# Letting the scheduler place two more elementwise steps on VectorE or GpSimd

## The chip, the cores and the metric

The kernel runs on one core of one Trainium2 chip. The metric is the device time of one execution in microseconds (us). The kernel before takes 389.71 us, the median of three runs (388.98 to 390.6). The profiled execution spans 388.5 us from its first to its last record, and all times read from the trace count from the start of that span.

The engines are named as in the profile: PE is TensorE, DVE is VectorE, ACT is ScalarE, POOL is GpSimd, and SP is the engine that issues most of the DMAs.

## The reference

Two parts follow each other. The first is attention in which a query sees only the keys of its own cluster. The second is a gated long convolution, computed in frequency space.

```python
# attention: B=4 batches, H=8 heads, S=768 positions, D=64
mask   = q_assign[:, :, :, None] == k_assign[:, :, None, :]   # nearest of 16 centroids
scores = scale * np.matmul(q, k.transpose(0, 1, 3, 2))
scores = np.where(mask, scores, -1e9)
attn   = softmax(scores)                                      # written out in the reference
x      = np.matmul(attn, v)                                   # heads joined to (B, S, 512)

# gated convolution ("hyena"), for each batch
proj = x @ w_proj                                             # 512 -> 3*512
x1, x2, x3 = proj[..., :D], proj[..., D:2*D], proj[..., 2*D:]
x2_conv = irfft(rfft(x2) * rfft(filter))                      # the spectral product
y = x1 * x2_conv * x3                                         # the product with the gates
out = y @ w_out
```

## The kernel before

The kernel doesn't write its instructions in program order. It first collects some 1,900 operations in a plan, each with the engines it may run on and a planned duration for each of them, with what it reads and writes and with a due time. A list scheduler then sends out the operations: it takes, for each engine, the operation that can start soonest, and among those that can start at about the same time the one with the earliest due time. The order in which operations are taken is the order of the instructions on each engine.

```python
def op(self, eng, fn, due, r=(), w=(), alloc=None, free=(), lock=False, ...):
    o.eng = eng if isinstance(eng, dict) else {eng[0]: eng[1]}    # {"POOL": 1.45, "DVE": .68} or ("DVE", .68)
    o.due += NUDGE.get(o.seq, 0.0)                                # a hand-set shift of single due times
    ...
```

An operation that may run on more than one engine has a dict of engines. `lock=True` marks the ones that the scheduler never lets overlap between DVE and POOL, in either direction:

```python
# place(): in choosing
if o.lock and e in ("POOL", "DVE"):
    t = late = max(t, st.dve if e == "POOL" else st.pool)
...
    c[1].due - (bonus if e == "PE" and st.kind == "pv" == c[1].kind else 0.0)
    + (shape if e == "PE" and array(c[1], st.last) != st.last else 0.0)
    + (BUSY if e == "DVE" and len(c[1].eng) > 1 else 0.0)         # DVE takes shared work later
...
# done(): after choosing
if e == "POOL" and o.lock: st.pool = t + d
if e == "DVE"  and o.lock: st.dve  = t + d
```

The attention is done in 16 passes, two for each of eight groups of four heads. A pass has six steps: PE makes scores, ACT takes their exponentials into one of five `p` buffers, PE multiplies with `v`, and DVE adds the exponentials up in `acc` for the softmax's denominators.

```python
op(("PE", 1.347), pv, due, r=[("p", slots[sk], u) for u in range(3)] + ..., w=[ob], kind="pv")
...
def acc(e, t=t):
    T.nc.vector.tensor_tensor(T.acc[os], P_(t[0]), P_(t[1]) if len(t) == 2 else T.acc[os], op=Alu.add)
op(("DVE", 1.75), acc, ..., w=[("acc", os)], lock=True)                          # L695
```

After most passes `acc` is folded from 128 rows to 16 by three DMAs that add on arrival. They are issued from POOL, one after the other. More DMAs then bring the sums into columns, DVE inverts them, and the inverses are spread to `rb`:

```python
while rows >= ROWS:
    op(("POOL", .8), lambda e, rows=rows: T.nc.gpsimd.dma_start(
        flat_()[:rows], flat_()[rows:2 * rows], accum_op=Alu.add), te, w=[("acc", os)], ...)   # L729
    rows //= 2
...                                                     # dd, dp, dn (DVE), dr, rb
op(("DVE", 1.05), ... scalar_tensor_tensor(xv(), osv(), eps(), rbv(), ...), w=[("xT", xs, kt)], lock=True)  # L775
```

Once a batch's `xT` is complete, its convolution ("hyena") is woven into the attention of later batches; that of the last batch comes after all attention. The parts that the change touches:

```python
def hyena(b):
    last = b == B - 1
    ...
    for i in range(3):
        for cs in range(2):                             # spectrum: PE into a bank h
            for r in range(2):                          # bank times filter, four products for each i
                op(("DVE", .68), ... tensor_tensor(T.tm[r][:, cs], ap(h), hmrow(...), op=Alu.mult), ...)     # L831
        for r in range(2):                              # sums of the spectral products
            op({"POOL": 1.45, "DVE": .68} if last and i < 2 else ("DVE", .68),
               lambda e, i=i, r=r: alu(e).tensor_tensor(
                T.y[:, i, r], T.tm[r][:, 0], T.tm[r][:, 1], op=Alu.add if r else Alu.subtract), due + 2,
               r=[("tm", r, 0), ("tm", r, 1)], w=[("y", i, r)], lock=True)                                    # L835
    ...
    for dt in range(4):
        ...                                             # gates on PE, x1 * x3 into x3 (ACT L260, DVE L871)
        ...                                             # inverse on PE, sums into sd (DVE L896), folded into yy (DVE L906)
        op(("DVE", .95), lambda e, dt=dt, x3=x3, yy=yy: alu(e).tensor_tensor(
            T.y2[:, dt], yy()..., x3()..., op=Alu.mult), due + 2.5, r=ykeys + xkeys,
            w=[("y2", dt)], lock=True)                  # L909, the product with the gates
    ...                                                 # y2 times w_out on PE, out to memory
```

There is one `tm[0]` and one `tm[1]`: the next products L831 can't be written before the sums L835 have read the last ones. `alu(e)` is the vector engine for "DVE" and GpSimd otherwise.

Of the kernel before, what the change touches and what calls it, by code (L numbers as in the profile page):

```python
# [22 lines left out]
B, H, S, D, NC = 4, 8, 768, 64, 16  # L23
# [9 lines left out]
NV = 3  # L33
NU = 4
ROWS = 16
LEAD = 1.97516
FIRST = 2
BUSY = 8.32578
HELD = 4
NUDGE = {10:3.7,75:-1.5,90:7.4,91:7.4,129:-0.8,140:0.4,156:6.6,187:-5.6,193:0.1,212:-0.2,216:15.5,218:8.0,222:-3.8,243:1.1,253:-4.1,255:-7.1,256:-7.1,257:-3.0,264:4.3,274:2.3,281:0.9,288:9.1,289:11.6,328:-9.2,363:0.5,370:2.2,378:0.5,379:0.7,400:-0.2,406:1.5,409:-4.8,434:0.6,440:-3.7,479:0.8,480:-0.3,481:-1.3,494:-0.6,495:-4.2,508:-1.9,511:-0.2,518:-5.0,524:0.5,526:2.1,539:-2.3,554:10.5,568:1.6,573:0.4,587:-4.9,590:0.2,597:-2.4,617:0.7,620:-1.0,658:0.8,664:0.1,684:2.2,690:-8.8,740:1.0,759:0.5,767:0.4,779:-0.7,782:1.7,788:0.7,790:0.8,826:-0.5,828:-0.3,848:-2.2,872:-1.3,883:-5.3,888:-3.6,897:-0.8,898:-1.1,901:-3.5,915:-3.1,941:0.4,947:-0.4,969:-0.8,996:2.0,997:2.0,1026:2.7,1029:-2.1,1039:2.0,1043:-1.2,1048:1.2,1056:10.8,1062:0.4,1066:0.9,1098:-1.0,1101:0.3,1118:-2.2,1127:1.5,1130:-1.5,1143:-2.6,1194:-0.9,1255:0.7,1257:0.7,1263:0.3,1270:-0.2,1271:-1.1,1276:-3.6,1295:4.9,1317:-2.0,1321:0.4,1351:5.6,1373:-1.5,1441:9.4,1450:3.5,1461:2.0,1478:-1.3,1501:-8.3,1546:0.2,1557:0.1,1563:-0.6,1624:2.8,1630:-1.5,1634:0.3,1640:-4.0,1641:-4.0,1642:-13.7,1643:-4.0,1655:-4.1,1666:0.5,1685:-2.9,1771:-3.3,1776:0.2,1788:-7.8,1797:0.1,1808:-0.1,1809:-0.1,1827:-0.7,1841:-1.3,1844:0.9,1862:-0.4,1863:2.1,1887:2.4,1890:3.2,1898:-7.4,1901:-0.8,1902:-1.5,1903:-0.8,1904:-0.8,1905:-1.8,1906:-1.8}  # L40
THIRDS = [[(0, 0, 512)], [(0, 512, 768), (1, 0, 256)], [(1, 256, 768)]]
HOLD = {"score": "score", "o": "o"}
AFTER = {"PE": .16}
# [32 lines left out]
class Plan:  # L76
# [6 lines left out]
    def op(self, eng, fn, due, r=(), w=(), alloc=None, free=(), lock=False, byts=0, after=(), kind=None, lat=0.0):  # L83
        o = Op()
        o.eng = eng if isinstance(eng, dict) else {eng[0]: eng[1]}
        o.fn, o.due, o.alloc, o.free, o.lock, o.byts, o.kind = fn, due, alloc, free, lock, byts, kind
        o.seq = len(self.ops)
        o.due += NUDGE.get(o.seq, 0.0)
        o.outs, o.end, o.start, o.on = [], None, None, None
        deps, o.soft = set(after), set(after)  # L90
        o.lat = lat
        for key in r:
            deps.update(self.writers.get(key, ()))
        for key in w:
            deps.update(self.writers.get(key, ()))
            deps.update(self.reads.get(key, ()))
        for key in r:
            self.reads.setdefault(key, []).append(o)
        for key in w:
            self.writers[key] = [o]  # L100
            self.reads[key] = []
        deps.discard(o)
        o.deps = deps
        o.left = len(deps)
        for d in deps:
            d.outs.append(o)
        for h in free:
            h.readers += 1
        self.ops.append(o)
        return o  # L110

    def place(self, free0, banks_for, switch=0.1, wait=0.1, rate=215e3, bonus=11.03330, margin=0.02203, shape=1.60501):
        free = dict(free0)
        bank_free = [0.0] * 8
        ready = {e: [] for e in free}
# [57 lines left out]
        while any(ready.values()):  # L173
# [28 lines left out]
            _, e, o, t = best  # L202
# [40 lines left out]
def build(T):  # L243

    P = Plan()
    op = P.op
    T0 = 20.36576
    TAU1 = 2.98452
    TAU2 = 3.43320
    NE = 28  # L250

    def ring(n, pr):
# [2 lines left out]
    def A(i):  # L255
        return T0 + TAU1 * min(i, NE) + TAU2 * max(i - NE, 0)

# [23 lines left out]
    def alu(e):  # L281
        return T.nc.vector if e == "DVE" else T.nc.gpsimd
# [253 lines left out]
    def routing(n):  # L536
        V = lambda: T.nc.vector
        g = n % 2
        end = A(12 * n)
        beg = A(12 * (n - 1)) if n else 0  # L540
        cls = "fill" if n > 1 else "head"
        for u in range(8):
# [7 lines left out]
            if n > 1 and ch == 0:  # L550
# [6 lines left out]
                for c in range(2):  # L557
                    op(EV384, lambda e, z=z, c=c, h=h: copy(e, T.qkT[z][:, c], bank(h.ids[c])[:, :384]), due + .9,
                       r=[h], w=[("qkT", z, c)], free=[h])
# [9 lines left out]
            if ch == 1:  # L569
                for hp in range(2):  # L570
# [3 lines left out]
                       r=[("qkT", z, 0), ("qkT", z, 1), ("zero", ring(n, pr), j)],  # L574
                       w=[("aug", ring(n, pr), hp, j)], lock=True)
        if n == 0:
            return got + first_masks(1)
        b0 = end - 24.00965
        h = Bank(cls, 2)

        def sim(e, h=h):
# [20 lines left out]
        for ch in range(2):  # L602
# [6 lines left out]
                op=Alu.is_equal), b0 + 3.4 + .2 * ch, r=[h, ("mx", ch)], w=[("oh", ch)], free=[h])  # L609
# [11 lines left out]
        for j, o_ in ((1, Alu.is_equal), (0, Alu.subtract)):  # L621
# [7 lines left out]
           r=both("oh"), w=both("ohT"), byts=196e3, lat=1.0)  # L629
# [153 lines left out]
    def hyena(b):  # L783
        xs = b % 2
        last = b == B - 1
        w0 = A(24 * (b + 1)) + 11.85069
        w1 = A(24 * (b + 2)) + 50.52404 if b < B - 2 else A(96) + 34.73131
        if last:
            w0 = A(96) - 8.47659
            w1 = w0 + 10  # L790
        acc = [0.0]

# [30 lines left out]
        for i in range(3):  # L823
            for cs in range(2):
                h = Bank()
                due = step(.66)
                op(("PE", .648), lambda e, i=i, cs=cs, h=h: spectrum(ap(h), i, cs), due,
                   r=[("uv2", e_, m) for m in range(3) for e_ in ((i,) if i < 2 else (0, 1))] + [("fw", m, cs) for m in range(3)],
                   w=[h], alloc=h, kind="proj" if i < 2 else "half")
                for r in range(2):  # L830
                    op(("DVE", .68), lambda e, i=i, cs=cs, r=r, h=h: T.nc.vector.tensor_tensor(  # L831
                        T.tm[r][:, cs], ap(h), hmrow(i, (0, 2, 2, 3)[2 * r + cs]), op=Alu.mult), due + 1 + .1 * r,
                       r=[h, ("hm", i, ((0, 2), (2, 3 if i == 0 else 0))[r][cs])], w=[("tm", r, cs), ("tm", r)], free=[h])
            for r in range(2):
                op({"POOL": 1.45, "DVE": .68} if last and i < 2 else ("DVE", .68), lambda e, i=i, r=r: alu(e).tensor_tensor(  # L835
                    T.y[:, i, r], T.tm[r][:, 0], T.tm[r][:, 1], op=Alu.add if r else Alu.subtract), due + 2, r=[("tm", r, 0), ("tm", r, 1)],
                   w=[("y", i, r)], lock=True)
        if last:
            op(("ACT", .83), lambda e: T.nc.scalar.activation(T.neg, T.inv[:, 1], Act.Copy, scale=-1.0), A(80),
               r=INV, w=["neg", ("qkraw", 0, 0), ("qkraw", 0, 1)])  # L840
        gs, inv = [], []
        for dt in range(ND):
            if last:
                x3, xkeys = (lambda dt=dt: T.qkT[dt][:]), [("qkT", dt, ch) for ch in range(2)]
            else:
                x3, xkeys = (lambda xb=dt % 2: T.x3[xb][:]), [("x3", dt % 2, ch) for ch in range(2)]
            if last and dt % 2:
                yy, ykeys = (lambda: T.sim[:].rearrange("p a (b c) -> p (a b) c", c=128)), [
                    ("sim", ch, pr) for ch in range(2) for pr in range(2)]
                od, okeys = (lambda: T.rb[:, :384]), [("rb", 0), ("rb", 1)]  # L850
            else:
                yy, ykeys = (lambda: T.yy[:]), [("yy", 0), ("yy", 1)]
                od, okeys = (lambda: T.od[:]), ["od"]
            sd, skeys = (lambda: T.sd[:]), [("sd", 0), ("sd", 1)]
            for ch in range(2):
                for off in (2 * DM, 0):
# [10 lines left out]
                    if off:  # L867
                        op(EV384, lambda e, ch=ch, x3=x3, h=h: copy(e, x3()[:, ch], ap(h)[:, :384]), due + .8,
                           r=[h], w=[xkeys[ch]], free=[h])
# [29 lines left out]
            for s_, o_ in ((0, Alu.add), (1, Alu.subtract)):  # L899
                def fold(e, s_=s_, o_=o_, yy=yy, sd=sd, hh=hh, od=od):  # L900
# [5 lines left out]
                    T.nc.vector.tensor_tensor(o[:, ::-1, 1, ::-1, ::-1] if s_ else o[:, :, 0], x[0], x[1], op=o_)  # L906
                op(("DVE", .55), fold, due + 2, r=[hh] + okeys if last else skeys, w=ykeys[s_::2], lock=not last,
                   free=[hh] if last else [])
            op(("DVE", .95), lambda e, dt=dt, x3=x3, yy=yy: alu(e).tensor_tensor(  # L909
                T.y2[:, dt], yy().rearrange("p t c -> p (t c)"), x3().rearrange("p a b -> p (a b)"),  # L910
                op=Alu.mult), due + 2.5, r=ykeys + xkeys, w=[("y2", dt)], lock=True)
        for tt in range(3):
# [261 lines left out]
```

The softmax here doesn't subtract the row's maximum and nothing guards it: scores larger than these inputs give would overflow.

## Time and profile before

| engine | busy us | share of the span | instructions |
|---|---|---|---|
| PE, matmuls | 369.0 | 95% | 3256 |
| PE, weight loads (beside the matmuls) | 214.3 | 55% | 3256 |
| DVE | 359.0 | 92% | 509 |
| ACT | 269.8 | 69% | 514 |
| POOL | 47.0 | 12% | 92 |

The TensorE clock is granted almost in full (0.998). Busy time is the union of an engine's instructions. A matmul's end is modelled, since matmuls overlap in the array, so the PE share says that matmuls were under way and not that the array was filled. The profile also follows one chain of work back from the end of the program; a piece of this chain is the work, or the wait, that the rest stood behind. Three stretches can be told apart: the start up to 20 us, attention with hyena woven in up to about 342 us, and after it the hyena of the last batch.

### The profile page before, as it was taken

What the parts mean: (1) busy time and instruction counts of PE and PEld (TensorE: products, weight loads), DVE (VectorE), ACT (ScalarE), POOL (GpSimd) and SP (SyncE); (2) the same over time, 40 slices, a digit from 0 to 9 for tenths busy, and PEclk for the clock granted to TensorE, in tenths of its full rate; (3) what the DMA queues carried; (4) which work ended last, traced back from release to release, by engine and by line L of the source; (5) the groups of instructions that cost most, each with busy time, mean ns of one, the idle gap of its engine ahead of it and who ended that gap; (6) DMA issues with size and microseconds to landing.
All of it is one profiled execution on the core that took longest, in us unless ns stands there. A gap on an engine that the chain in (4) does not pass through costs nothing.

```text
span 388.5 us, 8482 instructions
## 1 busy us (share of the span) xinstructions
PE 369.0 (95%) x3256; PEld 214.3 (55%) x3256; DVE 359.0 (92%) x509; ACT 269.8 (69%) x514; POOL 47.0 (12%) x92
## 2 busy tenths in 40 slices
PE   2999998999999999999999999999999999999995
PEld 1564454444445555555455554665454566557893
DVE  8898998899899999999899999999999999999782
ACT  5898687887884878787865976778865567632342
POOL 8502000000021010101010100101010100000400
PEclk9999999999999999999999999999999999999999
DMA  9819973740769759966897695745645651110214
GB/s 179 190 52 221 213 165 80 167 120 20 166 134 153 138 83 172 112 144 85 160 136 198 71 275 100 140 88 70 133 60 172 73 161 12 43 43 2 92 74 162
DMA packets 93860, 47.17 MB, mean 121 GB/s; under 512 B 82088, under 2 KB 87676, under 8 KB 93820
## 3 DMA queue, kind: packets, MB, share of 16 engines
q1 hardware_dynamic: 87836, 36.84, 41.6%
q0 software_dynamic: 2704, 8.98, 16.6%
q10 hardware_dynamic: 3280, 0.82, 1.2%
q8 instruction: 25, 0.41, 0.5%
q14 instruction: 15, 0.12, 0.1%
HBM read 31.59 MB, written 7.40 MB: 100 GB/s over the span
## 4 chain that ended last, share of the span: by engine, by line
PE 47%; DVE 35%; issue 7%; ACT 5%; DMA 3%; SPq 0%; DVEq 0%; POOL 0%; ACTq 0%; POOLq 0%
PE bank L73 17%; DVE acc L695 14%; PE pair L681 14%; PE bank L807 5%; PE bank L71 4%; DMA rb<-dr 2%; DVE oh L607 2%; PE bank L555 2%; DVE aug L262 2%; ACT p L670 2%; DVE tm L831 1%; PE bank L584 1%; DVE x L871 1%; ACT aug L260 1%; DVE mx L605 1%
## 5 line engine op out<-in xcount | busy, mean ns | idle before, releaser
L681 PE MATMUL pair<-p,vraw 128*64 128x385 f32 x768 | 142.9, 490 | 0.0
L670 ACT ACTIVATE p<-bank 128x512 f32<-128x512 f32 x192 | 113.7, 610 | 34.8 <-PE bank L73 33.3
L695 DVE TENSOR_TENSOR acc<-p,acc 128x1536 f32<-128x1536 f32 x64 | 111.9, 1749 | 3.5 <-ACT p L670 1.3
L681 PEld LDWEIGHTS pair<-p,vraw 128*64 128x64 f32 x768 | 54.0, 136 | 49.8 <-issue 45.2
L73 PE MATMUL bank<-aug,aug 80*64 80x512 bf16 (+3 forms) x590 | 69.7, 327 | 3.4 <-DVE den L717 1.0
L667 ACT ACTIVATE p<-bank 128x512 f32<-128x512 f32 x96 | 58.6, 610 | 2.7 <-PE bank L73 1.5
L73 PEld LDWEIGHTS <-aug 80*64 80x64 bf16 (+1 forms) x590 | 34.9, 109 | 34.7 <-issue 22.6
L729 POOL DMA_DIRECT2D acc<-acc x30 | 24.0, 799 | 245.5 <-DVE acc L695 85.4
L73 PE MATMUL bank<-xT,wpj 128*64 128x384 bf16 x424 | 41.4, 326 | 0.0
L260 ACT COPY qkT<-bank 128x384 f32<-128x384 f32 x62 | 27.9, 496 | 13.7 <-PE bank L73 8.9
L73 PEld LDWEIGHTS <-wpj 128*64 128x64 bf16 x424 | 27.9, 109 | 12.5 <-issue 6.7
L73 PEld LDWEIGHTS <-y 128*64 128x64 bf16 x448 | 24.9, 110 | 9.1 <-issue 3.0
L695 DVE TENSOR_TENSOR acc<-p,p 128x1536 f32<-128x1536 f32 x16 | 28.0, 1750 | 2.0 <-ACT p L670 2.0
L831 DVE TENSOR_TENSOR tm<-bank,hm 128x512 f32<-128x512 f32 x44 | 27.6, 677 | 0.8 <-ACT p L670 0.5
L260 ACT CAST aug<-qkT 64x768 bf16<-64x768 f32 x29 | 24.0, 829 | 3.0 <-PE bank L73 2.6
L807 PE MATMUL bank<-wpj,xT 128*64 128x512 bf16 x192 | 21.8, 380 | 0.4 <-DVE xT L775 0.4
L73 PE MATMUL bank<-wout,y 128*64 128x512 bf16 x176 | 21.4, 379 | 0.2 <-DVE y L909 0.2
L71 PE MATMUL bank<-aug,aug 80*128 80x256 bf16 (+3 forms) x89 | 19.9, 321 | 0.7 <-DVE tm L831 0.4
L555 PE MATMUL bank<-ident,qkraw 128*128 128x128 f32 x144 | 19.8, 279 | 0.2 <-DVE oh L607 0.2
L555 PEld LDWEIGHTS bank<-ident,qkraw 128*128 128x128 f32 x144 | 15.6, 140 | 7.1 <-issue 5.3
L260 ACT COPY tm<-bank 128x512 f32<-128x512 f32 x14 | 8.1, 590 | 16.1 <-PE bank L807 11.6
L262 DVE CAST aug<-qkT 64x768 bf16<-64x768 f32 x31 | 17.5, 569 | 1.5 <-PE bank L73 0.9
(149 smaller groups left out, 440.6 us busy)
## 6 DMA issues: line engine op xcount, KB each, us to landing
vraw<-in_v_dram SPq DMA_DIRECT2D x16, 384.0 KB, 4.3
qkraw<-in_q_dram SPq DMA_DIRECT2D x30, 192.0 KB, 5.0
qkraw<-in_k_dram SPq DMA_DIRECT2D x30, 192.0 KB, 5.1
rb<-dr SPq DMA_DIRECT2D x30, 192.0 KB, 3.7
out_dram<-ob SPq DMA_DIRECT2D x11, 512.0 KB, 3.6
acc<-acc POOLq DMA_DIRECT2D x10, 384.0 KB, 4.8
acc<-acc POOLq DMA_DIRECT2D x10, 192.0 KB, 4.0
y<-in_moe_filter_fft_dram SPq DMA_DIRECT2D x4, 384.0 KB, 6.8
```

The source lines that it names most:

```text
L71: return T.nc.tensor.matmul(out, lhsT, rhs, start=start, stop=stop)
L73: T.nc.tensor.matmul(out[64 * i:64 * i + 64], lhsT[:, 64 * i:64 * i + 64], rhs, start=start, stop=stop)
L260: T.nc.scalar.copy(out, in_)
L262: (T.nc.vector if e == "DVE" else T.nc.gpsimd).tensor_copy(out, in_)
L555: T.nc.tensor.transpose(bank(h.ids[i // 3])[:, ts(i % 3, 128)], raw(s, i), T.ident)
L667: T.nc.scalar.activation(o, ap(h).rearrange("p (a b) -> p a b", a=2), Act.Exp, scale=0.125)
L670: T.nc.scalar.activation(flat(s)[:, lo:lo + 512], ap(h), Act.Exp, scale=0.125)
L681: T.nc.tensor.matmul(o[64 * hp:64 * hp + 64, ch, :385], T.vraw[vs][:, hp, sk * D:(sk + 1) * D], T.p[slots[sk]][:, hp, 384 * ch:384 * ch + ...
L695: T.nc.vector.tensor_tensor(T.acc[os], P_(t[0]), P_(t[1]) if len(t) == 2 else T.acc[os], op=Alu.add)
L729: op(("POOL", .8), lambda e, rows=rows: T.nc.gpsimd.dma_start(flat_()[:rows], flat_()[rows:2 * rows], accum_op=Alu.add), te, r=[], w=[("ac ...
L807: T.nc.tensor.matmul(ap(h)[64 * i:64 * i + 64], T.xT[xs][:, kt, c:c + 64], T.wpj[:, kt, DM:2 * DM], start=kt == 0, stop=kt == ND - 1)
L831: op(("DVE", .68), lambda e, i=i, cs=cs, r=r, h=h: T.nc.vector.tensor_tensor(T.tm[r][:, cs], ap(h), hmrow(i, (0, 2, 2, 3)[2 * r + cs]), op ...
```

## The change

Two kinds of operations get GpSimd as a second possible engine. These are the sums of the spectral products (L835), before only in the last batch, now in all others too, and the products with the gates (L909) in all batches but the last. The purpose is to take elementwise work off VectorE where GpSimd has time. The scheduler decides instance by instance, by its planned durations.

The scheduler's constants and the hand-set due times were set anew along with it. The list of shifted due times grows from 142 to 420 operations; 121 of the old entries keep their value. No computation is added or left out.

```diff
-LEAD = 1.97516
+LEAD = 2.11573
-BUSY = 8.32578
+BUSY = 9.78676
-NUDGE = {10:3.7,75:-1.5,90:7.4, ... (142 entries) }
+NUDGE = {10:3.7,11:0.5,19:3.3, ... (420 entries) }
-    def place(self, ..., bonus=11.03330, margin=0.02203, shape=1.60501):
+    def place(self, ..., bonus=11.38616, margin=0.02203, shape=1.67099):
-    T0 = 20.36576
-    TAU1 = 2.98452
-    TAU2 = 3.43320
+    T0 = 20.37328
+    TAU1 = 2.98605
+    TAU2 = 3.41134
-        b0 = end - 24.00965
+        b0 = end - 24.14381
-        w0 = A(24 * (b + 1)) + 11.85069
-        w1 = A(24 * (b + 2)) + 50.52404 if b < B - 2 else A(96) + 34.73131
+        w0 = A(24 * (b + 1)) + 11.20895
+        w1 = A(24 * (b + 2)) + 50.66493 if b < B - 2 else A(96) + 36.68989
-            w0 = A(96) - 8.47659
+            w0 = A(96) - 9.51087
...
-                op({"POOL": 1.45, "DVE": .68} if last and i < 2 else ("DVE", .68), lambda e, i=i, r=r: alu(e).tensor_tensor(
+                op({"POOL": 1.45, "DVE": .68} if last and i < 2 or not last else ("DVE", .68), lambda e, i=i, r=r: alu(e).tensor_tensor(
                     T.y[:, i, r], T.tm[r][:, 0], T.tm[r][:, 1], op=Alu.add if r else Alu.subtract), ...
...
-            op(("DVE", .95), lambda e, dt=dt, x3=x3, yy=yy: alu(e).tensor_tensor(
+            op({"DVE": .95, "POOL": 2.2} if not last else ("DVE", .95), lambda e, dt=dt, x3=x3, yy=yy: alu(e).tensor_tensor(
                 T.y2[:, dt], ...
```

## The prediction

> **What bounds the kernel now.** I read the page's busy lines and its 40 slices first, then the busy times by stretch, then the groups of instructions, and last the chain that ended last.
>
> ```profile
> PE 369.0 (95%) x3256; PEld 214.3 (55%) x3256; DVE 359.0 (92%) x509; ACT 269.8 (69%) x514; POOL 47.0 (12%) x92
> ...
> PE   2999998999999999999999999999999999999995
> PEld 1564454444445555555455554665454566557893
> DVE  8898998899899999999899999999999999999782
> ACT  5898687887884878787865976778865567632342
> POOL 8502000000021010101010100101010100000400
> ```
>
> Two engines are nearly full at once, PE and DVE, and POOL is nearly empty from 20 us on. The busy times by stretch (start and end in us, length, then busy us and instructions of PE, weight loads, DVE, ACT and POOL) say where there is room:
>
> ```profile
> 20.00:120.00 100.00, 96.47 (x774) 49.32 (x772) 91.38 (x114) 81.22 (x156) 5.25 (x8) 1.00 0.62 133
> 120.00:300.00 180.00, 176.73 (x1494) 98.61 (x1492) 174.42 (x242) 133.52 (x252) 20.77 (x26) 1.00 0.71 130
> 300.00:340.00 40.00, 40.00 (x396) 24.16 (x394) 38.35 (x54) 25.32 (x49) 1.52 (x2) 1.00 0.39 78
> 340.00:380.00 40.00, 39.59 (x498) 32.56 (x496) 35.88 (x60) 13.74 (x27) 5.01 (x4) 1.00 0.15 51
> ```
>
> The operations of the change run from 129 us, where the first sums stand, to 342 us. Up to 120 us PE stands idle for 3.5 us that this change can hardly reach. From 120 to 300 us PE stands idle for 180 - 176.7 = 3.3 us, and from 300 to 340 us not at all. That is the visible room. The chain shows that there is also hidden room. From 220 to 240 us PE is counted as busy for 20.00 of 20 us, and yet the chain runs over DVE there (start us, us, what):
>
> ```profile
> 225.14 0.68 DVE tm L831
> 225.82 1.67 DVE acc L695
> 227.48 1.20 DVE tm L831 x2
> 228.68 0.45 DVE y L835
> 229.13 0.07 issue
> 229.20 0.68 DVE y L835
> 229.88 0.59 DVE acc L695
> 230.47 1.00 issue
> ```
>
> So DVE does set the pace in places, and the sums L835 are among the pieces. Over the whole span the chain is 47% PE and 35% DVE, which is 136 us of DVE. A busy PE with the chain on DVE means that matmuls trickle and their modelled ends cover the gaps.
>
> **What the Trainium skill says.** "Perfetto Trace Analysis", Identifying the Most-Contended Engine, says that matmul busy time is no good measure of how near PE is to its limit, while occupancy is a fair one for VectorE. The trace agrees: PE reads 100% busy from 220 to 240 us with weight loads at 10.33 us of 20, against 32.56 us of 40 from 340 to 380 us. "GPSIMD Engine Reference", Performance versus the Vector engine, gives a two-input add as 1.96 times slower there. The trace has the same sum on both engines, 1272 ns against 676, a factor of 1.88. "SBUF — State Buffer", Who interferes with whom, says that a VectorE instruction with two SBUF inputs contends with a GpSimd instruction that reads SBUF, and that the second to start waits in full. Nothing in this trace shows that pair: the four sums on POOL lie beside products of DVE that read a bank, and these kept their 0.68 us. It matters here, since the additions into `acc` have two SBUF inputs.
>
> **The change part by part.** The order of the built program tells how many operations really move. Before, 4 sums stood on POOL; after it is 22, so 18 leave DVE. Of the 12 products with the gates outside the last batch 6 go to POOL. Casts of `aug` on DVE fall from 31 to 24 (they go to ACT), copies of `inv` from 4 to 2, and ten copies from banks come to DVE (3 of 512 columns, 7 of 384). The matmuls are the same, and the changes between column layouts of the array number 86 against 82. Durations from the groups (busy us, mean ns):
>
> ```profile
> L835 DVE TENSOR_TENSOR y<-tm 128x512 bf16<-128x512 f32 x20 | 13.0, 676 | 0.0
> L909 DVE TENSOR_TENSOR y<-yy,x 128x768 bf16<-128x768 f32 x12 | 11.5, 958 | 0.5
> L835 POOL TENSOR_TENSOR y<-tm 128x512 bf16<-128x512 f32 x4 | 5.0, 1272 | 49.8 <-DVE tm L831 49.8
> ```
>
> With the means of the same view for the casts and copies, DVE loses 18 x 0.676 = 12.2 us of sums, 6 x 0.958 = 5.7 us of products, 7 x 0.569 = 4.0 us of casts and 2 x 0.25 = 0.5 us of `inv`: 22.4 us. It gains 3 x 0.692 + 7 x 0.541 = 5.9 us. Net DVE goes from 359.0 to about 342.5 us. POOL gains 18 x 1.27 = 22.9 us and, at 1.27/512 us a column, 6 x 1.9 = 11.4 us: 47 + 34 = 81 us. ACT gains 7 x 0.83 = 5.8 us of casts and gives back about as much in copies.
>
> What of the 17 us is on the path? The moved kinds have these larger pieces in the chain: sums 0.66 us at 129, 0.45 and 0.68 us at 229, 0.60 us at 317; products 0.96 us at 172, 0.97 us at 292, 0.64 us at 325. That is 5.0 us. Nearly all sums move and half of the products, so I count the sums in full (2.4 us) and half of the products (1.3 us): 3.7 us. The other 13 us lie beside PE's work; they only let a later addition into `acc`, an evacuation or a cast start sooner. PE's room caps what that can bring: 3.3 us visible from 120 to 300 us plus some hidden, and I count 2 us for it, my choice.
>
> Against it: a sum on POOL ends 1.27 - 0.68 = 0.6 us later and a product 1.9 - 0.96 = 0.95 us later. Each of three batches waits for its last sum before its inverse transform and for its last product before the output matmul. If half of this is covered, it is 3 x (0.6 + 0.95) / 2 = 2.3 us of delay on PE inputs, but PE has attention to do meanwhile, so I count 0.8 us. And where a POOL instruction meets an addition into `acc`, one waits: 24 times a chance that the schedule mostly avoids; I count 0.5 us. Sum: 389.7 - 3.7 - 2.0 + 0.8 + 0.5 = 385.3 us.
>
> **Rivals.** First, nothing moves, since PE is the bound. For it speaks that PE is 95% busy and full from 300 to 340 us, and that the attention's additions into `acc` (two groups of 111.9 and 28.0 us) stay on DVE. Against it speaks the chain on DVE. It would give 388 to 390 us. Second, a new wait on POOL: the three folding DMAs of `acc` are issued from the same POOL queue, in order, and in the new order sums stand between a first fold and its second, waiting for DVE's products. The folds, the spreading and `xT` then come later; the chain already holds 2% of the span in the wait for `rb`. Together with the shared port this could cost 2 to 6 us: 391 to 395 us. Against it: `acc` has two buffers, and the scheduler plans both the queue and the lock. Third, the 278 newly shifted due times are what really pays: the order is repacked everywhere, up to 120 us too. Then the gain could reach the whole idle time of PE in the middle and part of the hidden: 380 to 382 us. The shifts can't be priced from a profile of the old order; that they come with a shorter planned step (TAU2 3.411 for 3.433) says only that the order is meant to be tighter.
>
> **Range and chances.** The cap is PE: 369 us busy plus what nothing fills, 7.8 us in the first 20 and 4.4 us in the last 8.5, makes 381.2 us unless hidden gaps close as well. Faster by over 2% needs less than 381.9 us, nearly the cap, and so gets 0.16. Slower by over 2% needs 397.5 us, beyond the second rival: 0.04. The rest is 0.80. The range is 380.5 to 390.0 us: the third rival below, the first above.
>
> **What would show it.** Right: DVE near 342 us busy and POOL near 80; PE busy within 3 us of 369 with less idle time from 120 to 300 us; hardly any L835 among the chain's pieces before 342 us; additions into `acc` still near 1.75 us. Wrong: additions into `acc` or sums on POOL clearly longer than 1.75 and 1.27 us (the port); more time waiting for `rb` or for POOL (the queue); a gain that lies mostly before 120 us, or a PE busy time lower by over 4 us (the repacked order, and hidden gaps larger than I count).

## The result, and the profile after

The changed kernel takes 394.24 us (median; 393.62 to 396.57), the kernel before 389.92 us in the same set of runs. The ratio is 1.0123 with a 95% interval of 1.0077 to 1.017: about 1.2% slower, where the prediction had 385.3 us and a range of 380.5 to 390.0. The profiled execution spans 392.6 us against 388.5.

The page's busy lines and three of its 40-slice lines:

```profile
PE 370.1 (94%) x3281; PEld 210.1 (54%) x3281; DVE 354.8 (90%) x485; ACT 273.1 (70%) x514; POOL 85.5 (22%) x116
...
PE   2999998999999999898999999999998999999995
...
DVE  8898998896999999979999899999996999999882
...
POOL 8501100000020741401010350401021170501500
```

The move took place: DVE has 24 instructions fewer and POOL 24 more, and POOL's busy time rose by 38.5 us. But DVE's busy time fell only from 359.0 to 354.8 us. The prediction's count of instructions would have taken it to about 342.5. The busy times by stretch (columns as before: start:end, length, then busy us and instructions of PE, weight loads, DVE, ACT and POOL) show that PE did not close its gaps either:

```profile
20.00:120.00 100.00, 96.98 (x775) 52.18 (x773) 89.43 (x108) 83.89 (x162) 5.13 (x8) 1.00 0.61 133
120.00:300.00 180.00, 174.81 (x1494) 98.80 (x1492) 170.67 (x226) 134.69 (x249) 44.19 (x40) 1.00 0.68 125
300.00:340.00 40.00, 38.08 (x374) 21.27 (x372) 35.73 (x48) 22.92 (x44) 11.69 (x10) 1.00 0.46 100
340.00:380.00 40.00, 39.88 (x501) 26.16 (x497) 36.51 (x58) 14.32 (x29) 10.05 (x6) 1.00 0.14 51
```

From 120 to 300 us PE stands idle for 5.2 us (3.3 before), from 300 to 340 us for 1.9 us (none before). The attention's last pass ends on PE at 346.2 us instead of 342.3; what follows takes as long as before (46.4 and 46.2 us). So the loss lies where the moved operations lie, between 120 and 342 us.

The groups of instructions tell where DVE's relief went (busy us and mean ns of one after the bar, then the idle time before them and what ended it):

```profile
L695 DVE TENSOR_TENSOR acc<-p,acc 128x1536 f32<-128x1536 f32 x64 | 116.9, 1826 | 3.7 <-ACT p L670 1.1
...
L695 DVE TENSOR_TENSOR acc<-p,p 128x1536 f32<-128x1536 f32 x16 | 30.1, 1880 | 4.4 <-ACT p L667 3.9 <-ACT p L670 0.4
...
L835 POOL TENSOR_TENSOR y<-tm 128x512 bf16<-128x512 f32 x22 | 29.6, 1372 | 23.5 <-DVE tm L831 23.5
...
L775 DVE SCALAR_TENSOR_TENSOR xT<-osb,rb 128x768 bf16<-128x768 f32 x15 | 16.7, 1115 | 5.2 <-DMA rb<-dr 5.2
...
L909 POOL TENSOR_TENSOR y<-yy,x 128x768 bf16<-128x768 f32 x6 | 15.1, 2524 | 41.6 <-DVE yy L906 27.6 <-PE bank L807 14.0
...
L740 DVE TENSOR_SCALAR dn<-dn 128x12 f32<-128x12 f32 x10 | 4.7, 468 | 0.3
```

Before, the same groups of DVE were:

```profile
L695 DVE TENSOR_TENSOR acc<-p,acc 128x1536 f32<-128x1536 f32 x64 | 111.9, 1749 | 3.5 <-ACT p L670 1.3
...
L695 DVE TENSOR_TENSOR acc<-p,p 128x1536 f32<-128x1536 f32 x16 | 28.0, 1750 | 2.0 <-ACT p L670 2.0
...
L775 DVE SCALAR_TENSOR_TENSOR xT<-osb,rb 128x768 bf16<-128x768 f32 x15 | 15.1, 1006 | 1.3 <-DMA rb<-dr 1.3
...
L740 DVE TENSOR_SCALAR dn<-dn 128x12 f32<-128x12 f32 x10 | 1.7, 173 | 0.3
```

The same instructions on the same data now last longer: 7.0 us more for the additions into `acc`, 3.0 us for L740, 1.6 us for L775, together 11.5 us. A mean hides the form of this: most of these instructions are as long as before, and 13 single ones carry the whole 11.5 us (8 of the 80 additions, 4 of L740, 1 of L775). Each of them starts while an elementwise operation stands on POOL. The timeline around 230 us (start us, us, engine, line) shows two such meetings:

```profile
227.77 1.31 DVE L831 TENSOR_TENSOR tm<-bank,hm 128x512 f32<-128x512 f32 x2
...
228.85 1.50 POOL L835 TENSOR_TENSOR y<-tm 128x512 bf16<-128x512 f32 x1
228.99 2.98 DVE L695 TENSOR_TENSOR acc<-p,p 128x1536 f32<-128x1536 f32 x1
231.89 0.68 DVE L831 TENSOR_TENSOR tm<-bank,hm 128x512 f32<-128x512 f32 x1
...
232.74 1.27 POOL L835 TENSOR_TENSOR y<-tm 128x512 bf16<-128x512 f32 x1 [2.40 <-DVE tm L831]
232.96 2.67 DVE L695 TENSOR_TENSOR acc<-p,acc 128x1536 f32<-128x1536 f32 x1
```

The sum on POOL runs from 232.74 to 234.01 us. The addition of 232.96 ends at 235.63, that is 1.62 us after the sum has ended, against 1.75 us for an undisturbed addition: it stood still behind the sum and then ran nearly as if it began there. The products L831 read a bank, and keep their 0.68 us beside POOL. The case of 292 us is the clearest. L740 works on 12 elements a row and takes 0.17 us alone:

```profile
292.49 1.82 POOL L909 TENSOR_TENSOR y<-yy,x 128x768 bf16<-128x768 f32 x1 [7.15 <-DVE yy L906]
292.77 1.56 DVE L740 TENSOR_SCALAR dn<-dn 128x12 f32<-128x12 f32 x1
```

It ends at 294.33 us, just after the product has ended at 294.31. The chain of waits shows the price of the second addition (start us, us, what):

```profile
233.03 0.59 DVE acc L695
233.63 1.92 issue
```

In the chain of before, shown with the prediction, the same pair of pieces was 0.59 and 1.00 us. The second has grown by 0.92 us, and this addition lasts 0.92 us longer than the mean of before. The blocked time is not named: it goes under "issue", the time for which the profile shows no reason.

### The profile page after: what moved, and what is told of

It reads as the page before. It is cut to its first block, busy times and chain, and to the rows that moved or that the text cites. A ratio compares the mean times of both kernels' runs of the same rounds, so it can differ in the third digit from the quotient of the medians.

```text
span 392.6 us, 8528 instructions
## 1 busy us (share of the span) xinstructions
PE 370.1 (94%) x3281; PEld 210.1 (54%) x3281; DVE 354.8 (90%) x485; ACT 273.1 (70%) x514; POOL 85.5 (22%) x116
## 4 chain that ended last, share of the span: by engine, by line
PE 70%; DVE 16%; ACT 5%; DMA 4%; issue 3%; SPq 1%; POOL 0%; DVEq 0%; POOLq 0%; ACTq 0%
PE bank L73 27%; PE pair L681 24%; PE bank L807 5%; PE bank L71 3%; DVE acc L695 3%; PE bank L555 3%; DMA rb<-dr 2%; PE bank L584 2%; DVE oh L607 2%; PE bank L450 2%; ACT p L670 1%; DVE mx L605 1%; DMA dp<-dd 1%; PE bank L565 1%; PE bank L709 1%
## 5 line engine op out<-in xcount | busy, mean ns | idle before, releaser
L670 ACT ACTIVATE p<-bank 128x512 f32<-128x512 f32 x192 | 111.6, 606 | 29.2 <-PE bank L73 26.5
L695 DVE TENSOR_TENSOR acc<-p,acc 128x1536 f32<-128x1536 f32 x64 | 116.9, 1826 | 3.7 <-ACT p L670 1.1
L73 PE MATMUL bank<-aug,aug 80*64 80x256 bf16 (+3 forms) x584 | 68.9, 327 | 4.3 <-DMA aug<-ohT 1.8
L667 ACT ACTIVATE p<-bank 128x512 f32<-128x512 f32 x96 | 58.1, 606 | 5.7 <-PE bank L73 5.1
L835 POOL TENSOR_TENSOR y<-tm 128x512 bf16<-128x512 f32 x22 | 29.6, 1372 | 23.5 <-DVE tm L831 23.5
L695 DVE TENSOR_TENSOR acc<-p,p 128x1536 f32<-128x1536 f32 x16 | 30.1, 1880 | 4.4 <-ACT p L667 3.9
L73 PEld LDWEIGHTS <-wpj 128*64 128x64 bf16 x424 | 24.4, 109 | 15.9 <-issue 6.9
L260 ACT CAST aug<-qkT 64x768 bf16<-64x768 f32 x36 | 29.8, 830 | 3.0 <-PE bank L73 1.2
L831 DVE TENSOR_TENSOR tm<-bank,hm 128x512 f32<-128x512 f32 x44 | 27.7, 680 | 1.7 <-POOL y L835 0.7
L909 POOL TENSOR_TENSOR y<-yy,x 128x768 bf16<-128x768 f32 x6 | 15.1, 2524 | 41.6 <-DVE yy L906 27.6
L71 PE MATMUL bank<-aug,aug 128*128 128x512 bf16 (+3 forms) x92 | 20.6, 323 | 1.8 <-DVE x L262 1.0
L775 DVE SCALAR_TENSOR_TENSOR xT<-osb,rb 128x768 bf16<-128x768 f32 x15 | 16.7, 1115 | 5.2 <-DMA rb<-dr 5.2
```

The source lines that it names most:

```text
L71: return T.nc.tensor.matmul(out, lhsT, rhs, start=start, stop=stop)
L73: T.nc.tensor.matmul(out[64 * i:64 * i + 64], lhsT[:, 64 * i:64 * i + 64], rhs, start=start, stop=stop)
L260: T.nc.scalar.copy(out, in_)
L667: T.nc.scalar.activation(o, ap(h).rearrange("p (a b) -> p a b", a=2), Act.Exp, scale=0.125)
L670: T.nc.scalar.activation(flat(s)[:, lo:lo + 512], ap(h), Act.Exp, scale=0.125)
L835: op({"POOL": 1.45, "DVE": .68} if last and i < 2 or not last else ("DVE", .68), lambda e, i=i, r=r: alu(e).tensor_tensor(T.y[:, i, r], T. ...
```

## The experiments

One theory (the port theory) stood against three rivals. The theory: GpSimd's reads of SBUF block DVE, and the blocking eats the relief. The rivals: the new order of instructions is at fault; or the fuller POOL queue delays the folds of `acc` and so `rb`; or the relief of DVE is worth nothing in itself because PE or another wait takes over. Every ratio below is against the kernel before in the same set of runs, without the executions that took over 1.5% longer than the fastest of their kernel.

### Reads or writes on GpSimd, in the new order

The order and the engines of every instruction are those of the changed kernel. The 24 moved operations are replaced by two fills, which only write, between two reads of a single column. The sums and products themselves are left out.

```diff
+def wonly(e, o, x, z, f):                       # o = x f z
+    if last or e == "DVE": return alu(e).tensor_tensor(o, x, z, op=f)
+    n = o.shape[-1]
+    T.nc.gpsimd.tensor_tensor(o[:, :1], x[:, :1], z[:, :1], op=f)
+    for _ in range(2): T.nc.gpsimd.memset(o[:, 1:n - 1], 0.0)
+    T.nc.gpsimd.tensor_tensor(o[:, n - 1:], x[:, n - 1:], z[:, n - 1:], op=f)
-    alu(e).tensor_tensor(T.y[:, i, r], ...)     # L835, and L909 likewise
+    wonly(e, T.y[:, i, r], ...)
```

> The changed kernel in its own order, but each of the 24 moved operations on GpSimd is replaced by a read of one column, two writes of a constant over the rest, and a read of the last column. The queue stays as occupied and the waits stay; only the long reads of SBUF by GpSimd are gone, and with them the sums and products themselves. Port theory (GpSimd's reads and VectorE's two-input instructions hold each other up): additions into acc back to 1750 ns in the mean, the 11.5 us of lengthened VectorE instructions gone, time 385 to 389 us. Queue theory (operations on GpSimd delay the folding DMAs behind them): nothing changes, 392 to 396 us. Order theory (the newly set due times are themselves worse on the chip): nothing changes, 392 to 396 us.

Measured: 392.4 us, a ratio of 1.0037 (1.0014 to 1.0059). The profiled execution is a quick one of this kernel (its span is 387.5 us), so its trace is used for durations only. DVE is busy for 345.0 us, within 2.5 us of what the prediction's count said. The port theory's time, 385 to 389 us, was missed; its lengths came out. The additions are back at their old length although POOL, at 90.8 us, is even busier:

```profile
L695 DVE TENSOR_TENSOR acc<-p,acc 128x1536 f32<-128x1536 f32 x64 | 112.0, 1750 | 5.7 <-ACT p L670 3.3
```

Its timeline near the same place shows a fill beside an addition:

```profile
226.28 1.23 POOL L803 MEMSET y<- 128x510 bf16 x2
226.57 1.75 DVE L695 TENSOR_TENSOR acc<-p,p 128x1536 f32<-128x1536 f32 x1
227.47 0.91 POOL L804 TENSOR_TENSOR y<-tm 128x1 bf16<-128x1 f32 x1
...
229.00 0.19 POOL L801 TENSOR_TENSOR y<-tm 128x1 bf16<-128x1 f32 x1 [0.63 <-DVE tm L840]
```

The addition of 226.57 us overlaps the fills and takes 1.75 us. The read of one column that follows the fills, 0.19 us when alone, takes 0.91 us: it waits for the end of the addition at 228.32. Of the 11.5 us of lengthening, 0.8 us is left: four of the ten L740 still take 0.30 to 0.58 us beside fills (a mean of 254 ns for 173). So fills spare the additions, not every DVE instruction. The two ratios, 1.0123 and 1.0037, have intervals that don't overlap; their difference, 0.86% or 3.4 us, is what the long reads of SBUF on GpSimd cost. "SBUF — State Buffer", Who interferes with whom, of the Trainium skill says exactly this: a VectorE instruction with two SBUF inputs contends with a GpSimd instruction that reads SBUF and not with one that only writes, and the second to start is blocked in full. These runs agree: beside a read an addition took 2.98 us, beside fills 1.75.

### The new order with everything on VectorE

```diff
-alu(e).tensor_tensor(T.y[:, i, r], ...)                               # L835, and L909 likewise
+(alu(e) if last else T.nc.vector).tensor_tensor(T.y[:, i, r], ...)
```

The order is again that of the changed kernel; the moved operations stand at their planned places, on DVE.

> The changed kernel with every instruction where it stands, but the 24 moved operations are issued on VectorE at the same place of the order. Port theory: VectorE gets 17 us of work back and loses 11.5 us of stalls, so 392 to 396 us, with the additions at 1750 ns. Queue theory: the folds start as soon as their data are there, 387 to 391 us. Order theory: VectorE is now fuller than the order was made for, 396 to 402 us.

Measured: 396.7 us, 1.0169 (1.0132 to 1.0205), just above the port theory's 392 to 396 us and within the order theory's range; DVE 358.6 us busy, additions 1749 ns. So in this order the relief is worth something: from 1.0169 to 1.0037 it is 1.3%, 5.1 us, if it is had without the blocking. With it 0.5% is left (1.0123), and the intervals overlap. But this order was made for 24 instructions less on DVE. Against the kernel before, the order with its relief and without the blocking is still not ahead.

### The new constants and due times alone

```diff
-LEAD = 1.97516; BUSY = 8.32578; NUDGE = {... 142 entries}; TAU2 = 3.43320; ...
+LEAD = 2.11573; BUSY = 9.78676; NUDGE = {... 420 entries}; TAU2 = 3.41134; ...
```

The engine options stay those of before; the scheduler makes a new order.

> All constants and shifted due times of the changed kernel, but the sums and products may only go where they could before, so the scheduler makes a new order with them on VectorE. Port and queue theories: no loss remains, 386 to 390 us. Order theory: the loss remains, 393 us or more.

Measured: 404.06 us, 1.0356 (1.0313 to 1.0399). Two lines of its busy times by stretch:

```profile
340.00:380.00 40.00, 35.76 (x451) 27.87 (x448) 33.21 (x53) 9.69 (x20) 5.01 (x4) 0.96 0.04 11
380.00:402.00 22.00, 13.82 (x112) 6.47 (x108) 8.01 (x12) 6.04 (x11) 0.00 (x0) 0.88 0.37 144
```

The last pass ends on PE at 343.0 us, within a microsecond of the kernel before. The loss lies almost all behind it, where the last batch's operations take 58.0 us instead of 46.2, PE is idle for 4.2 of 40 us, and the granted clock (the column after POOL's) is lower. That is a place that the options don't touch. The run therefore doesn't weigh the new due times for the changed kernel. It shows only that the scheduler's order with these due times and the old engines is slow in another place.

### The two options alone

```diff
-{"POOL": 1.45, "DVE": .68} if last and i < 2 else ("DVE", .68)
+{"POOL": 1.45, "DVE": .68} if last and i < 2 or not last else ("DVE", .68)   # L835
-("DVE", .95)
+{"DVE": .95, "POOL": 2.2} if not last else ("DVE", .95)                      # L909
```

Constants and due times stay those of before. The scheduler puts 17 more sums and 6 products on POOL.

> The kernel before with its own constants and due times; only the two operations may go to GpSimd as in the change (21 sums and 6 products end there). Port theory: VectorE instructions are lengthened by 8 to 13 us in all, 391 to 396 us. Queue theory: 391 to 396 us, with a longer wait for rb. Order theory: no loss, 385 to 389 us.

Measured: 394.5 us, 1.0108 (1.0076 to 1.014), as slow as the full change. The lengthening is there again (1838 ns for the first additions, 1119 for L775, 469 for L740), with an order that shares neither constants nor due times with the changed kernel. It comes to about 6 us, less than the 8 to 13 expected; but DVE's products L831 here also wait 4.0 us for POOL to read `tm` (0.3 us before), so this run does not set the two apart.

### The old order, writes only and real

The order of the kernel before is kept to the instruction. The 18 sums of the first three batches and every second product are issued on POOL at their places: once as fills, as above (sums and products left out), and once in earnest.

```diff
-alu(e).tensor_tensor(T.y[:, i, r], ...)                        # L835
+wonly(e if last else "POOL", T.y[:, i, r], ...)                # fills
-alu(e).tensor_tensor(T.y2[:, dt], ...)                         # L909
+wonly(e if last or dt % 2 else "POOL", T.y2[:, dt], ...)
```

The second kernel has `alu(e if ... else "POOL").tensor_tensor` in place of `wonly`.

> The order of the kernel before on every engine, untouched; its 18 sums of the first three batches and 6 of the products leave VectorE and become, on GpSimd, the read of one column, two writes of a constant and the read of the last column. VectorE is relieved by 18 x 0.676 + 6 x 0.958 = 17.9 us and the port is left alone; the sums and products are left out. If relief is worth something in the old order (the prediction's step): 385 to 388 us. If PE or the order leave no room for it: 389 to 391 us.

> The order of the kernel before on every engine, untouched; the same 18 sums and 6 products are really computed on GpSimd. Port theory: VectorE instructions are lengthened by 10 to 16 us in all, since this order was not made for it (most sums are followed by an addition into acc), and the time is 3 to 6 us above that of the kernel with writes only in the old order: 390 to 395 us. If the newly set order is the cause of the loss and not the port: 385 to 388 us.

Measured: 390.92 us for the fills, 1.0009 (0.9989 to 1.003), and 395.12 us in earnest, 1.015 (1.0091 to 1.021). The blocking costs 1.4%, about 5.5 us, in the old order; the additions last 1812 and 1844 ns and L775 1189 ns.

The first of these is the more telling one. The fills take 14 us off DVE's busy time and leave the additions alone, and the time stays where it was. Its busy line, and the 120 to 300 us of its busy times by stretch:

```profile
PE 368.5 (95%) x3256; PEld 206.7 (53%) x3256; DVE 345.0 (89%) x485; ACT 269.8 (69%) x514; POOL 88.7 (23%) x188
```

```profile
120.00:300.00 180.00, 176.06 (x1492) 97.16 (x1488) 164.45 (x226) 132.94 (x252) 48.04 (x90) 1.00 0.69 128
```

DVE is busy for 164.45 us of the 180 instead of 174.42, and PE for 176.06 instead of 176.73. The 10 us of relief became 10 us of idle time. DVE's waits name more than half of it. Over the whole span, before and with the fills (what waited, for what: us in all, times, longest):

```profile
DVE tm L831 <- POOL y L835: 0.3, 1, 0.3
...
DVE tm L840 <- POOL y L804: 8.8, 9, 1.4
```

L840 and L804 are the products L831 and the last read of a sum in the file of this kernel. There is one `tm`, so after each of the nine groups of sums DVE's next products wait until POOL has read it. In this order, which has those products close behind, 8.8 of the 14 us came back as a wait for POOL; 5.8 of them fall between 120 and 300 us. With the real sums the wait is 8.1 us, so the comparison of the two kernels still shows the blocking. In the changed kernel it is 0.7 us.

The shares of the chain, before, by engine:

```profile
PE 47%; DVE 35%; issue 7%; ACT 5%; DMA 3%; SPq 0%; DVEq 0%; POOL 0%; ACTq 0%; POOLq 0%
```

With the fills:

```profile
PE 61%; DVE 23%; issue 4%; ACT 3%; DMA 3%; POOL 2%; SPq 1%; DVEq 0%; POOLq 0%; ACTq 0%
```

DVE lost 12 points of the chain and PE gained 14, at the same time. POOL's 2% are the fills themselves: 4.7 us from 128 us on and 2.7 us from 310 us on, where the chain of before had 0.66 and 0.60 us of sums on DVE. The first piece is a read of one column (0.19 us alone) that ends just after an addition of DVE from 128.78 to 130.52 us:

```profile
128.35 2.23 POOL y L801
```

So this order shows what the move is worth in it even without blocked additions, nothing, and not what 14 us less on DVE would be worth if nothing else had become late.

DVE's wait for `rb` is 3.7 us here against 1.3 before. Without the waits for `rb`, further down, the kernel with fills is 0.5% faster (1.0009 to 0.996) and the one without them 0.2%. So a price of the fuller queue is not ruled out. For the changed kernel the fills show that 3.4 us of its loss go while the queue stays as full.

### One kind at a time, in the new order

```diff
-alu(e).tensor_tensor(T.y2[:, dt], ...)          # products back on DVE: sums alone move
+alu("DVE").tensor_tensor(T.y2[:, dt], ...)
-alu(e).tensor_tensor(T.y[:, i, r], ...)         # second kernel: sums back, products alone move
+alu(e if last else "DVE").tensor_tensor(T.y[:, i, r], ...)
```

> The order of the changed kernel; the sums stay on GpSimd, the 6 products go back to VectorE at their places. Port theory: 6 x 1.82 us of GpSimd reads less, which lengthened VectorE by 0.71 + 0.71 + 1.39 + 0.55 + 1.57 = 4.9 us, against 5.7 us of work that comes back: about the changed kernel's time, 393 to 396 us. If the products on GpSimd are what is late: 389 to 392 us.

> The order of the changed kernel; the 6 products stay on GpSimd, the 18 sums go back to VectorE. Port theory: 6.6 us of lengthening go and 12.2 us of work come back: 394 to 398 us. If the sums on GpSimd, between the folding DMAs, are what is late: 389 to 392 us.

Measured: sums alone 393.27 us, 1.0082 (1.0053 to 1.0112); products alone 396.15 us, 1.017 (1.0126 to 1.0214). The sums block the additions most (1796 and 1880 ns); the products account for all of L775's lengthening (1116 ns; 1011 with the sums alone). Moving the products alone is no better than moving nothing in this order (1.0169). Neither kind is a gain on the kernel before.

### What paces the old order

If the relief brings nothing because PE is the bound, it should pay once PE has less to do. The next kernels take work off PE: three batches leave out two of the four terms of their output product.

```diff
 def W(e, kts=range(ND), ...):
-    for kt in kts:
+    for kt in kts if last else (0, ND - 1):
```

The first has everything else as before; the second adds the fills on POOL.

> The kernel before, with every other engine untouched; TensorE leaves out two of the four terms of the output product in the first three batches (18 times 4 of 8 matmuls). In the trace of before 8 of them take 1.03 us next to each other, and pairs follow at 0.22 us, so about 18 x 0.43 = 7.8 us of TensorE work go. TensorE theory (it alone paces, which is why VectorE's relief brings nothing): 383 to 385 us. Shared pace (TensorE and VectorE take turns, either alone brings little): 388 to 391 us.

> The same TensorE work left out, and VectorE relieved by the 24 operations as in the old order with writes only. TensorE theory: no better than with the TensorE work left out alone, 383 to 385 us. Shared pace: only both together pay, 380 to 385 us, 4 us or more below the other.

Measured: 388.73 us, 0.9963 (0.9936 to 0.999), and 388.9 us, 0.9963 (0.9945 to 0.998). PE's busy time falls by 6.5 us to 362.5, and 1.4 us come through. The fills on top add nothing, and 388.9 us is above what either theory had for them (380 to 385 us). So PE alone is not the one bound either. DVE's wait of 8.8 us for POOL is there again, as in all kernels below that have the fills.

The other suspect in the chain is the wait for `rb`. Here `rb` is spread once, for the first pass; later passes use those old values, so the normalization of all other passes is left out.

```diff
 for hp in range(2):
-    op(("SP", .6), lambda e, hp=hp: T.nc.sync.dma_start(
+    op(("SP", .6), lambda e, hp=hp: (n or pr) or T.nc.sync.dma_start(
         T.rb[64 * hp:64 * hp + 64], T.dr[os][hp:hp + 1].to_broadcast([64, S])), ...)
```

Alone, with the fills, with the shorter output product, and all three together:

> The kernel before in its own order; the DMAs that spread the inverse denominators to rb are issued for the first pass alone, so 14 later passes use the old rb and wait for no rb (the normalization is left out, all else stays). Chain theory (what paces is the chain of DMAs from a pass's sums to xT, before which TensorE in its fixed order waits; relief of an engine can't help): 383 to 387 us. Packed-order theory (every engine's fixed order holds the others; no single thing removed pays more than 2 us): 388 to 390 us.

> The same, with VectorE relieved of 17.9 us by writes only on GpSimd. Chain theory: with the chain gone VectorE's relief pays at last, 379 to 384 us, 3 us or more below the kernel without relief. Packed-order theory: 387 to 390 us.

> The kernel before in its own order, with half of the output product's terms left out on TensorE in three batches (about 7.8 us of TensorE work) and rb spread for the first pass alone; VectorE untouched. Packed theory (TensorE, VectorE and the rb DMAs are all near the pace): VectorE is left as the pace, 386 to 389 us. Other theory (loads, masks or something else paces): the same, 386 to 389 us.

> The same, and VectorE relieved of 17.9 us by writes only on GpSimd. Packed theory: now all three give way and the time falls to 378 to 383 us, 4 us or more below the run without VectorE's relief. Other theory: 385 to 389 us.

Measured, with the ratio to the kernel before:

| taken away | us | ratio | interval |
|---|---|---|---|
| DVE's moved work (fills) | 390.92 | 1.0009 | 0.9989 to 1.003 |
| `rb` | 389.84 | 0.9983 | 0.9968 to 0.9998 |
| part of PE's work | 388.73 | 0.9963 | 0.9936 to 0.999 |
| `rb`, DVE's | 389.17 | 0.996 | 0.9942 to 0.9979 |
| PE's, DVE's | 388.9 | 0.9963 | 0.9945 to 0.998 |
| PE's, `rb` | 388.11 | 0.9938 | 0.9917 to 0.9958 |
| all three | 386.4 | 0.9903 | 0.9873 to 0.9932 |

Each alone brings at most 0.4%, all three together 1.0%, more than the sum of the single effects (0.45%). The busy line and the chain's shares of the last kernel:

```profile
PE 361.3 (94%) x3183; PEld 201.6 (52%) x3188; DVE 344.7 (89%) x485; ACT 269.1 (70%) x514; POOL 90.5 (24%) x188
...
PE 62%; DVE 29%; issue 3%; POOL 3%; ACT 1%; DVEq 0%; POOLq 0%; ACTq 0%
```

Nearly 8 us are off PE and 14 off DVE's busy time (8.8 of them again waits for POOL, which has 3% of this chain), and the wait for `rb` is gone from the chain, yet only 3.8 us of time went. The theory of a packed order, in which each of these holds the others, was put at 378 to 383 us and isn't met in size: the mark of 385 to 389 held. With PE and `rb` relieved, the fills move the ratio from 0.9938 to 0.9903; those intervals overlap, so even that last 0.35% isn't certain. What paces the kernel after that was not found. The first 110 us, which none of these three touches much, are nearly alike in these kernels: the fifth pass ends on PE between 109.2 and 110.9 us. What follows the last pass takes 43.8 to 47.0 us, 46.2 before.

## Why the prediction was wrong

**DVE's work: right.** The count of moved instructions gave 342.5 us for DVE and 81 us for POOL without blocking. (It has one copy from a bank too many, 0.5 us: the trace shows nine that come, not ten.) With fills DVE has 345.0 us, and POOL has 85.5 us in the changed kernel. A GpSimd product takes 1.82 us alone (estimated: 1.9), a sum 1.27. PE stayed within 3 us of 369.0, at 370.1.

**"24 times a chance that the schedule mostly avoids; I count 0.5 us": failed in size.** It measured 3.4 us in the new order and 5.5 us in the old. The mechanism had been named, and its mark was the right one: additions clearly longer than 1.75 us. The trace of before even showed it, against the prediction's "Nothing in this trace shows that pair". In the start, L319, which has two inputs in SBUF and 1 element a row, began just after a cast of GpSimd and lasted 0.78 us until that had ended. In the new order with everything on VectorE, where it begins before the cast, it takes 0.16 us. The cast in the timeline, and L319 as a piece of the chain:

```profile
8.60 0.82 POOL L262 CAST aug<-qkT 64x768 bf16<-64x768 f32 x1
8.65 0.79 DVE s L319
```

The failure was to trust the scheduler's `lock`. It keeps apart only the planned times. Two such instructions share no data, so the kernel has no wait between them, and where the real times differ from the plan they meet: 13 DVE instructions were caught. L740, which takes 0.17 us and carries no `lock`, was not considered at all; 3.0 of the 11.5 us lie there. The page of the skill that the prediction named has the rule; what had to be added was the number of meetings and what one costs, 0.9 us (11.5 / 13).

**"Sums in full (2.4 us) and half of the products (1.3 us): 3.7 us", and "2 us" for the rest: failed as a gain on the kernel before.** The pieces did leave the chain: of 5.0 us of sums and products there is one product of 0.96 us left, and no sum. The time did not leave with them. Without blocked additions the new order with its relief is 1.4 us slower than the kernel before (1.0037), where 5.7 us of gain were counted. Two things are shown about it. In the new order the relief itself is worth 5.1 us (1.0169 to 1.0037), but the same order with everything on DVE stands 6.6 us above the kernel before, and the sum gave the new order no term. In the old order the same move brings nothing (1.0009, 0.9989 to 1.003), and there DVE's products wait 8.8 us for POOL. The prediction let a later sum delay only PE's inputs, and not DVE's own next products, although they share `tm`. Why the new order, where that wait is 0.7 us, still gains nothing stays open. The first rival had the right size for this part, 388 to 390 us; that PE is the one bound was not shown.

**"0.8 us" for later sums and products: not seen in the changed kernel, far too small for the old order.** After the first 20 us no piece of the changed kernel's chain is POOL's. In the old order with the fills POOL has 7.3 us of it.

**The rivals.** The second had 391 to 395 us and holds the result, 394.24, but for half of its reason: of its two parts the shared port is shown, with 3.4 us, and the queue is not. The wait for `rb` did grow, from 1.3 to 5.2 us; with fills in the same order it is 3.6 us, and what it costs was not separated from the new order. The third, the order that pays (299 due times are new or changed, not 278), is refuted: with its relief and no blocking it is 0.4% behind.

**The sum, as measured.** The new order, its relief and its later sums together cost 1.4 us (1.0037) where a gain of 4.9 us was counted (5.7 less 0.8); the port cost 3.4 us where 0.5 were. Together 4.8 us, which is 1.23% of 389.9. Where the 1.4 us lie was not settled. The trace of the changed kernel has PE waiting 1.8 us for mask rows (`aug` from `ohT`) from 160 to 180 us (0.7 us before, and 1.8 us with the fills in the new order too); no experiment was made on it.

## What to carry to other kernels

Work moved from VectorE to GpSimd is not free where GpSimd's reads meet VectorE instructions that take two inputs from SBUF: count the meetings (here 0.9 us each, beside GpSimd operations of 1.27 to 1.82 us), and look for VectorE groups whose mean has grown after the move. A scheduler's rule that two operations shall not overlap does nothing on the chip unless a wait enforces it. An engine's share of the chain is no measure of a gain: replace the moved work with fills in the same order first, and then read the waits of that kernel. Here this shows at once that the move gains nothing in the old order, and that 8.8 of the 14 us come back as a wait for the one `tm` buffer. "Perfetto Trace Analysis", Optimizing Scalar/DVE Operations, of the Trainium skill warns that moving work between these two engines might not help since they share a read port; here it agreed, at a cost of 0.9 to 1.4%.

## What the runs showed of the hardware

- A VectorE operation on 12 elements a row (`TENSOR_SCALAR`, from SBUF to SBUF) is blocked until the GpSimd operation ends: beside a product at 292.77 us it took 1.56 us for 0.17 us. Fills hold it up too, though not the additions: 0.58 us at 139.65 us in the new order with fills. A cast of DVE from SBUF to SBUF (L262, 0.57 us in the mean) took 1.10 us beside fills in the old order and 2.18 us beside a real product. L740's neighbour L739, a `TENSOR_REDUCE` on the same rows, isn't blocked: it took 0.48 us at 140.18 us, wholly beside a sum on POOL, and 0.50 us at 164.16 us with no elementwise work there.
- The blocking goes both ways, and shows as length in either case: an addition 3.08 us for 1.75, a GpSimd product 3.28 us for 1.82, a GpSimd sum 2.80 us for 1.27. Blocked time counts as busy, so the busy share of an engine can rise or hold while its work falls.
- VectorE products that read a bank aren't blocked: L831 has a mean of 680 ns after and 677 ns before, though some run beside sums on POOL.
